# A retention and maxout kernel on one core: the first FFN products moved around block 3 of the start-up

## The chip, the cores and the metric

The kernel runs on one core of a Trainium2 chip. The metric is the device time of one execution in microseconds (us); the figure for a kernel is the median of its runs. Engines are named as in the profile: PE is TensorE (PEld its weight loads), DVE is VectorE, ACT is ScalarE, POOL is GpSimd, SP is SyncE, whose queue issues most of the transfers.

## The reference

Eight sequences of 576 tokens with eight heads of 64 go through causal retention (attention with a decay in place of the softmax); the result, 4608 tokens of 512 values, goes through a feed-forward network whose hidden layer is the maximum of three products.

```
scores = scale * q @ k^T                         # per batch and head
ret    = scores * (gamma ** (i - j) if i >= j else 0)
x      = (ret @ v), heads side by side           # 4608 x 512, float32
h      = max(x @ w1, x @ w2, x @ w3)             # w: 512 x 768, float64 from the host
out    = h @ w_out                               # 4608 x 512
```

## The kernel before

**Retention by blocks.** The 36 blocks of 128 tokens are worked through in order. For a block, `load(g)` fetches k, q and v; `decay(g)` multiplies v by the key decay on GpSimd (L249); `transposes(g)` makes kT and qT, for the first seven blocks by TensorE (L271) with a copy from PSUM by ScalarE (L272), later by VectorE; `scores(g)` is kT x qT on TensorE (L285) with a causal mask on VectorE; `state(g)` and `keep(g)` carry the sum of k x v from block to block (L352, L362, L363); `values(...)` is scores x v (L393) plus the part from the state (L406), scaled by the output factors `gq` and written to `xT` by VectorE. Blocks 8 and later use chunks of 64 tokens instead (L307, L310).

**The FFN by tiles of four blocks.** Tile t has 512 tokens (NT), `xT[t]`. The first tile is computed with plain products: `up_plain` (L784) is one of 18 products of 128 hidden columns, each with four sub-products over the depth; `i` = 0 is copied to `h` by ScalarE (L789), i = 1 and 2 are combined by a maximum on VectorE (L788). `downs_plain` (L771) is the output product. Later tiles use sums and differences of operands that save products (L748, L760, L557).

**Weights.** They come as 64-bit floats. `load_weights(1)` fetches one piece (128 hidden columns, 512 KB, two transfers; L499) into half of a `bits` buffer. `convert(n)` takes n steps of a generator that turns pieces into 32-bit floats, in steps named exponent, fraction, whole, sign and product, of which exponent and fraction have ScalarE parts (L632, L638, L641) and all have VectorE parts (L630, L639, L644, L648, L656). The first piece takes four steps, the second four. For the next pairs, up to the sixth piece, exponent and fraction of both pieces come before whole, sign and product. `product` ends by fetching one more piece.

**Order.** The schedule is manual: each engine gets its instructions in program order. At the end of the kernel's body the first four blocks stand written out by hand, with conversion steps between them; then, for every tile, a list of steps for the next tile's blocks alternates with parts of the FFN. From the second tile on, VectorE work for the coming blocks goes through a queue, `urgent`; the FFN takes entries from it at certain steps (L839, L840), and `scores` and `values` empty it before they begin. The hand-written order of loads at the start is:

```
k0 q0 v0  k1 q1 v1  (state factors gs)  k2 q2 v2  k3 q3  w0  v3  w1  k4 q4 v4  w2 w3 w4 w5
```

Of the kernel before, what the change touches and what calls it, by code (L numbers as in the profile page):

```python
# [45 lines left out]
ALU = mybir.AluOpType  # L46
PSUM = bass.MemoryType.PSUM

C = 128
NT = 4 * C  # L50
# [27 lines left out]
WAHEAD = 6  # L78
# [3 lines left out]
def kernel(  # L82
# [14 lines left out]
    nc = tc.nc  # L97
    P = 128
    B, H, S, D = q.shape
# [4 lines left out]
    NDC = DM // P  # L104
    NF = DF // P
    CPT = NT // C
# [8 lines left out]
    ppool = ctx.enter_context(tc.tile_pool(name="ppool", bufs=PARTS))  # L115
    opool = ctx.enter_context(tc.tile_pool(name="opool", bufs=2))
    while_converting = ExitStack()
    wraw = while_converting.enter_context(tc.tile_pool(name="wraw", bufs=WAHEAD // 2))
    wtmp = while_converting.enter_context(tc.tile_pool(name="wtmp", bufs=2))
    raw0 = while_converting.enter_context(tc.tile_pool(name="raw0", bufs=1))  # L120
    ps_r = ctx.enter_context(tc.tile_pool(name="ps_r", bufs=4, space=PSUM))
# [3 lines left out]

    gk = const.tile([C, H], FP32, name="gk")
    gs_of = const.tile([P, H], FP32, name="gs_of")
    gs = const.tile([P, NP], FP32, name="gs")  # L130
    one, top, inf, first = (const.tile([P, 1], FP32, name=n) for n in ("one", "top", "inf", "first"))
    const.tile([P, FILL // 4], FP32, name="fill")
    gq = const.tile([P, NP, C], FP32, name="gq")
    nc.scalar.dma_start(gk[:], key_decay)
    nc.vector.memset(one[:], 1.0)
    nc.scalar.copy(first[:], one[:])

# [11 lines left out]
    def warm(n):  # L149

        ps = ps_y.tile([P, P], FP32, tag="y", name="warm")
        for _ in range(n):
            nc.tensor.matmul(ps[:], lhsT=ident[:], rhs=ident[:], start=True, stop=True)
# [15 lines left out]
    def spans(g):  # L169

        row = 0
        while row < C:
# [1 line left out]
            n = min(C - row, S - pos)  # L174
            yield row, b, pos, n
            row += n

    def half(j):
        return slice(D * j, D * (j + 1))

    def place(g, c):

# [39 lines left out]
                        t[r:r + 32, :, e, :],  # L222
                        src[b, :, pos:pos + 32, 32 * a:32 * a + 32].rearrange("h p i -> p h i"))

    def load(g):
        if g >= BY_PE and ("q", g) not in raws:
            load_blocks(g, *range(C // 32))
        for n, src in (("k", k), ("q", q), ("v", v)) if g < BY_PE else (("k", k), ("v", v)):
            if n == "v" and g == CPT - 1:
                load_weights(1)  # L230
            bufs = {"k": 3, "q": 2, "v": 4}[n]
            pool, bufs = (raw0, 1) if n != "v" and g < BY_PE and g % (bufs + 1) == bufs else (raw, bufs)
            if n == "v":
                t = vpool.tile([C, H, D], FP32, tag="v", name="vraw")
            else:
                t = pool.tile([C, H, D], FP32, tag=n, name=n + "raw", bufs=bufs)
            raws[n, g] = t
            for row, b, pos, m in spans(g):
                nc.sync.dma_start(t[row:row + m], src[b, :, pos:pos + m, :].rearrange("h p d -> p h d"))
# [100 lines left out]
    def state_factors():  # L340
        for j in range(2):
            nc.scalar.copy(gs_of[half(0), j::2], gs[half(j)])
# [386 lines left out]
    def convert(n):  # L729
        for _ in range(n):  # L730
            next(converting, None)
# [44 lines left out]
                    nc.sync.dma_start(out[t * NT + m * P:t * NT + (m + 1) * P, :], osb[:])  # L776
            yield

    def up_plain(t, h, fb, i):
        ps = (ps_x, ps_y)[fb % 2].tile([P, NT], FP32, tag="xy"[fb % 2], name="up")  # L780
        first_of_all = t == 0 and (fb, i) == (0, 0)
        for cols in (slice(0, NT - C), slice(NT - C, NT)) if first_of_all else (slice(0, NT),):
            for dc in range(NDC):
                nc.tensor.matmul(ps[:, cols], lhsT=w_sb[i, fb][:, dc * P:(dc + 1) * P], rhs=xT[t][:, dc, cols],  # L784
                                 start=dc == 0 and cols.start == 0, stop=dc == NDC - 1,
                                 skip_group_check=first_of_all)
        if i > 0:
            return lambda: nc.vector.tensor_tensor(h[:, fb, :], h[:, fb, :], ps[:], op=ALU.max)  # L788
        return lambda: nc.scalar.copy(h[:, fb, :], ps[:])  # L789

    def ffn(t):

        h = hpool.tile([P, NF, NT], FP32, tag="h", name="h")
        if t == 0:
            for fp, i in units:
                for fb in (2 * fp, 2 * fp + 1):
                    maximum = up_plain(t, h, fb, i)
                    if CPT not in qks:
                        maximum()
                        transposes(CPT)  # L800
                        convert(4)
                        continue
                    if (fp, i) == units[-1]:
                        maximum()
                        convert(2)
                        continue
                    convert(4 if (fp, i) in units[:2] else 2)
                    maximum()
                yield
            convert(3)  # L810
            for fb, _ in enumerate(downs_plain(t, h)):
                convert(2 if fb < 2 else 4 * len(pieces))
                if fb == 2:
                    while_converting.close()
                    late["pool"] = ctx.enter_context(tc.tile_pool(name="late", bufs=1))
                    late_room()
                    sums_of_outs()
                elif fb > 2:
                    chore({3: 4, 4: 0, 5: 2}[fb])
                if fb in (1, 3):  # L820
                    yield
            yield
            return
        if t == 1:
            spread.append(True)
            weight_sums(0)
            weight_sums(2)
        plain = 1 if t == 1 else None
        order = (1, 0, 2) if t == 1 else (0, 2, 1)
        total = sum(48 if fp == plain else 2 * len(PRODUCTS) for fp in order)  # L830
        count = parts = 0
        for fp in order:
            if fp != plain:
                while fp not in summed_fp:
                    chore()
            for step, cost in enumerate(up_plain_all(t, h, fp) if fp == plain else up(t, h, fp)):
                if fp == plain:
                    chore(4 if step == 4 else 8)
                elif step % 4 == 1 or step % 4 == 3 and len(urgent) > 6:  # L839
                    chore(len(urgent) > 0)  # L840
                elif step % 4 == 2 and chores and (t > 1 or NF // 2 - 1 not in summed_fp):
                    chores.popleft()()
                if step % 3 == 2:
                    scale()
                count += cost or 1
                if count * (NF // 2 * 3) >= (parts + 1) * total:
                    parts += 1
                    yield
            sums_of_hidden(h, fp)
            if fp == plain:  # L850
                weight_sums(fp)
        chore(len(urgent))
        for n, _ in enumerate(downs(t, h, order)):
            chore(4)
            scale(2)
            if n in (1, 3):
                yield
        yield

    def up_plain_all(t, h, fp):  # L860
        for fb in (2 * fp, 2 * fp + 1):
            for i in range(3):
                up_plain(t, h, fb, i)()
                yield 8


    warm(6)
    for g in range(CPT):
        load(g)
        if g == 1:  # L870
            for j in range(2):
                nc.sync.dma_start(gs[half(j)].unsqueeze(2), state_decay[half(j), :, D * j:D * j + 1])
    load_weights(1)
    load(CPT)
    load_weights(4)
    decay(0)
    transposes(0)
    for c in range(2):
        for b in range(2):
            nc.scalar.dma_start(gq[half(c), b::2, :], out_decay[half(b), NP // 2 * c:NP // 2 * (c + 1), :])  # L880
    warm(2)
    scores(0)
    transposes(1)
# [4 lines left out]
    scores(1)  # L888
    first_output()
    transposes(2)  # L890
    state_factors()
    decay(2)
    state(1)
    keep(1)
    values([1], [1])
    transposes(3)
    decay(3)
    scores(2)
    scores(3)
    state(2)  # L900
    keep(2)
    convert(2)
    values([2], [2])
    convert(2)
    values([3], [3])
    convert(4)
    keep(3)
    decay(CPT)
    convert(2)

    def steps(t):

# [11 lines left out]
        if t == 1:  # L924
            a, b, c, d = range(CPT, 2 * CPT)
            at(0, (load, b))
            at(1, (scores, a), (state, a), (keep, a))
            at(2, (transposes, b), (decay, b), (load, c))
            at(3, (scores, b), (load_blocks, d, 0))
            at(4, (decay, c), (load_blocks, d, 1, 2))  # L930
            at(5, (values, [a, b], [b, c]), (load_blocks, d, 3), (load, d))
            at(6, (keep, c), (transposes, c), (load_blocks, d + 1, 0))
            at(7, (transposes, d), (decay, d), (load_blocks, d + 1, 1, 2))
            at(8, (scores, c), (scores, d), (load_blocks, d + 1, 3), (load, d + 1))
            at(9, (load_blocks, d + 2, 0, 1))
            at(10, (decay, d + 1), (load_blocks, d + 2, 2))
            at(11, (values, [c, d], [d]), (load_blocks, d + 2, 3), (load, d + 2),
               (transposes, d + 1))
            return todo
# [70 lines left out]
```

## Time and profile before

| | |
|---|---|
| Time, median of 3 | 756.83 us (756.58 to 757.96) |
| Profiled span | 754.8 us |
| TensorE busy | 745.0 us |
| VectorE busy | 509.2 us |
| ScalarE busy | 320.0 us |
| GpSimd busy | 83.3 us |
| First FFN product begins | 25.97 us |
| Granted TensorE clock | 1.00 |

Times in the profile count from the span's start. A line of the timeline has the start, the time to the end of the group, the engine, the line of the kernel, the operation with output and inputs, and how many instructions are joined; in square brackets stands how long the engine was idle before, and who released it. A line of the waits has the total in us, how often, and the longest.

### The profile page before, as it was taken

What the parts mean: (1) busy time and instruction counts of PE and PEld (TensorE: products, weight loads), DVE (VectorE), ACT (ScalarE), POOL (GpSimd) and SP (SyncE); (2) the same over time, 40 slices, a digit from 0 to 9 for tenths busy, and PEclk for the clock granted to TensorE, in tenths of its full rate; (3) what the DMA queues carried; (4) which work ended last, traced back from release to release, by engine and by line L of the source; (5) the groups of instructions that cost most, each with busy time, mean ns of one, the idle gap of its engine ahead of it and who ended that gap; (6) DMA issues with size and microseconds to landing.
All of it is one profiled execution on the core that took longest, in us unless ns stands there. A gap on an engine that the chain in (4) does not pass through costs nothing.

```text
span 754.8 us, 16567 instructions
## 1 busy us (share of the span) xinstructions
PE 745.0 (99%) x6728; PEld 608.2 (81%) x6728; DVE 509.2 (67%) x856; ACT 320.0 (42%) x645; POOL 83.3 (11%) x103
## 2 busy tenths in 40 slices
PE   8999999999999999999999999999999999999998
PEld 7645545588888888888888888888888888888887
DVE  2998896858876866677567647675667656763662
ACT  3574531064245443543355435542454245414441
POOL 3110112001000110011010101010101010100000
PEclk9999999999999999999999999999999999999999
DMA  9995842504241414342243324242415151000001
GB/s 218 254 216 125 234 98 69 100 2 77 66 102 40 85 44 100 56 73 55 69 88 63 65 61 95 33 81 63 87 38 96 43 97 32 1 30 29 0 1 56
DMA packets 230204, 59.30 MB, mean 79 GB/s; under 512 B 210800, under 2 KB 228848, under 8 KB 230128
## 3 DMA queue, kind: packets, MB, share of 16 engines
q1 hardware_dynamic: 229264, 57.91, 35.0%
q8 instruction: 53, 0.87, 0.5%
q10 hardware_dynamic: 864, 0.33, 0.2%
q14 instruction: 23, 0.19, 0.1%
HBM read 48.76 MB, written 9.44 MB: 77 GB/s over the span
## 4 chain that ended last, share of the span: by engine, by line
PE 96%; DVE 2%; DMA 1%; issue 0%; ACT 0%; POOL 0%; DVEq 0%; POOLq 0%
PE a L760 18%; PE b L760 15%; PE dx L557 11%; PE up L784 11%; PE c L760 8%; PE dz L557 5%; PE d L760 5%; PE e L760 5%; PE sk L307 3%; PE down L771 3%; PE dy L557 3%; PE o L424 2%; PE o L431 2%; PE s L285 1%; DMA qraw<-in_q_dram 1%; PE kv L310 1%
## 5 line engine op out<-in xcount | busy, mean ns | idle before, releaser
L748 DVE TENSOR_TENSOR part<-part 128x512 f32<-128x512 f32 x161 | 111.2, 691 | 108.4 <-ACT part L745 106.0
L745 ACT COPY part<-b 128x512 f32<-128x512 f32 x115 | 67.4, 586 | 154.8 <-PE b L760 154.8
L748 DVE TENSOR_TENSOR h<-h,part 128x512 f32<-128x512 f32 x115 | 80.3, 698 | 29.3 <-ACT h L745 25.4
L784 PE MATMUL up<-xT,w 128*128 128x512 f32 (+2 forms) x200 | 84.7, 578 | 1.5 <-DVE w L656 1.5
L745 ACT COPY part<-a 128x512 f32<-128x512 f32 x92 | 53.9, 586 | 49.0 <-PE a L760 48.5
L784 PEld LDWEIGHTS up<-xT,w 128*128 128x128 f32 x200 | 36.8, 190 | 43.5 <-issue 39.6
L760 PE MATMUL a<-s,w 128*128 128x256 f32 x276 | 70.9, 379 | 0.0
L760 PE MATMUL b<-s,n 128*128 128x256 f32 x276 | 70.8, 379 | 0.0
L189 ACT ACTIVATE vraw<-vraw,gk 128x64 f32<-128x64 f32 x208 | 65.7, 347 | 4.5 <-DMA vraw<-in_v_dram 4.4
L760 PEld LDWEIGHTS b<-s,n 128*128 128x128 f32 x276 | 52.4, 190 | 7.1
L760 PEld LDWEIGHTS a<-s,w 128*128 128x128 f32 x276 | 52.4, 190 | 7.1
L527 POOL TENSOR_TENSOR H<-h 128x256 f32<-128x256 f32 x24 | 20.2, 843 | 308.7 <-DVE h L748 308.7
L760 PE MATMUL c<-xT,w 128*128 128x256 f32 x184 | 49.1, 389 | 0.0
L760 PE MATMUL d<-s,w 128*128 128x256 f32 x184 | 47.3, 379 | 0.0
L760 PE MATMUL b<-xT,n 128*128 128x256 f32 x184 | 47.2, 379 | 0.0
L324 POOL TENSOR_TENSOR s<-s,gs_of 64x512 f32<-64x512 f32 x21 | 22.2, 1055 | 213.7 <-DVE s L322 209.1
L557 PE MATMUL dx<-To,H 128*128 128x256 f32 (+1 forms) x204 | 44.9, 370 | 0.0
L760 PE MATMUL e<-xT,w 128*128 128x256 f32 x184 | 43.5, 379 | 0.0
L760 PE MATMUL a<-xT,n 128*128 128x256 f32 x184 | 43.5, 379 | 0.0
L557 PEld LDWEIGHTS dx<-To,H 128*128 128x128 f32 x204 | 36.6, 190 | 4.9
L760 PEld LDWEIGHTS e<-xT,w 128*128 128x128 f32 x184 | 35.0, 190 | 5.2 <-DVE s L322 0.2
L760 PEld LDWEIGHTS d<-s,w 128*128 128x128 f32 x184 | 34.9, 190 | 4.9 <-ACT part L745 0.2
(122 smaller groups left out, 1287.2 us busy)
## 6 DMA issues: line engine op xcount, KB each, us to landing
bits<-in_moe_w_dram SPq DMA_DIRECT2D x36, 256.0 KB, 5.1
out_dram<-osb SPq DMA_DIRECT2D x35, 256.0 KB, 2.1
kraw<-in_k_dram SPq DMA_DIRECT2D x32, 256.0 KB, 3.0
vraw<-in_v_dram SPq DMA_DIRECT2D x32, 256.0 KB, 3.5
qraw<-in_q_dram SPq DMA_DIRECT2D x224, 32.0 KB, 2.1
kxraw<-in_k_dram SPq DMA_DIRECT2D x224, 32.0 KB, 2.1
bits<-in_moe_w_out_dram SPq DMA_DIRECT2D x6, 512.0 KB, 5.5
qraw<-in_q_dram SPq DMA_DIRECT2D x6, 256.0 KB, 5.2
```

The costliest lines, as they stand in the source:

```text
L189: scaling.popleft()()
L307: nc.tensor.matmul(s[half(c), h, :], lhsT=kT[half(c), h, :], rhs=qT[half(c), h, :], start=True, stop=True)
L324: nc.gpsimd.tensor_tensor(new, new, factor, op=ALU.mult)
L424: nc.tensor.matmul(o[m][half(c), n, u, :], lhsT=vds[g][half(m), h, :], rhs=sts[g][half(m), h, :], start=n == 0 and u == 0, stop=place(g, m ...
L431: nc.tensor.matmul(o[m][half(c), n, u, :], lhsT=stacks[g][half(m), h, :], rhs=qks[g]["q"][half(m), h, :], start=False, stop=True, skip_gro ...
L527: urgent.append(lambda: (pool(s3, a11, a21, op=ALU.subtract), pool(s4, a12, s2, op=ALU.subtract)))
L557: nc.tensor.matmul(o, lhsT=hS[n](fp)[:, m * P:(m + 1) * P], rhs=late["T"][n][:, fp, cols], start=first and fp == order[0] and (m == 0 or l ...
L745: nc.scalar.copy(of[step], ps[step[0]][:])
L748: nc.vector.tensor_tensor(of[dst], a, b, op=op)
L760: nc.tensor.matmul(ps[chain][:, e, :], lhsT=factor(w, 2 * fp + e), rhs=xS[t][x], start=n == 1 and e == 0, stop=ends, skip_group_check=True)
L771: nc.tensor.matmul(b[:], lhsT=h[:, fb, m * P:(m + 1) * P], rhs=w_sb["out", fb], start=(fb == 0), stop=(fb == NF - 1))
L784: nc.tensor.matmul(ps[:, cols], lhsT=w_sb[i, fb][:, dc * P:(dc + 1) * P], rhs=xT[t][:, dc, cols], start=dc == 0 and cols.start == 0, stop= ...
```

## The change

Part of the retention of block 3 is waited for at the start, and so is the first weight. The change loads the first two weight pieces before block 3's k and q and before its v, converts the first one during block 2, and puts the first 384 columns (tokens of blocks 0 to 2) of the first FFN product ahead of block 3's state and values and those of the second product behind them; the last 128 columns of both follow. The state factors are fetched on ScalarE's queue at the very beginning, and half of the output factors ahead of block 0's transposes. A fourth `bits` buffer takes two more pieces ahead. In the second tile, entries of `urgent` are taken at a further step while more than two are waiting (six before).

```diff
-    wraw = while_converting.enter_context(tc.tile_pool(name="wraw", bufs=WAHEAD // 2))
+    wraw = while_converting.enter_context(tc.tile_pool(name="wraw", bufs=WAHEAD // 2 + 1))
     nc.scalar.dma_start(gk[:], key_decay)
+    for j in range(2):
+        nc.scalar.dma_start(gs[half(j)].unsqueeze(2), state_decay[half(j), :, D * j:D * j + 1])
...
+    def first_ups(h):
+        g = CPT - 1
+        rest0, copy0 = up_plain(0, h, 0, 0, g * C)
+        convert(2)
+        state(g)
+        values([g])
+        keep(g)
+        rest1, copy1 = up_plain(0, h, 1, 0, g * C)
+        for step in (rest0, copy0, rest1, copy1):
+            step()
+        decay(CPT)
+        transposes(CPT)
+        convert(10)
...
-                elif step % 4 == 1 or step % 4 == 3 and len(urgent) > 6:
+                elif step % 4 == 1 or step % 4 == 3 and len(urgent) > (2 if t == 1 else 6):
...
-    for g in range(CPT):
+    for g in range(CPT - 1):
         load(g)
-        if g == 1:
-            for j in range(2):
-                nc.sync.dma_start(gs[half(j)].unsqueeze(2), state_decay[half(j), :, D * j:D * j + 1])
     load_weights(1)
+    load(CPT - 1, "kq")
+    load_weights(1)
+    load(CPT - 1, "v")
+    load_weights(2)
     load(CPT)
-    load_weights(4)
+    load_weights(2)
     decay(0)
+    output_factors(0)
     transposes(0)
+    output_factors(1)
...
     transposes(2)
-    state_factors()
     decay(2)
     state(1)
     keep(1)
     values([1], [1])
-    transposes(3)
-    decay(3)
     scores(2)
-    scores(3)
+    decay(CPT - 1)
     state(2)
     keep(2)
+    convert(3)
+    values([2], [2])
+    transposes(CPT - 1)
+    convert(1)
+    state_factors()
     convert(2)
-    values([2], [2])
-    convert(2)
-    values([3], [3])
-    convert(4)
-    keep(3)
-    decay(CPT)
-    convert(2)
+    scores(CPT - 1)
...
-            at(2, (transposes, b), (decay, b), (load, c))
+            at(2, (transposes, b), (decay, b), (load, c), (load_weights, 2))
```

In the old order the first tile's FFN began with the whole first product, then block 4's transposes, then the second product.

More of the change, by code (lines that the diff above doesn't have):

```diff
@@ L124, with half @@
     ctx.enter_context(tc.manual_schedule())
+    def half(j):
+        return slice(D * j, D * (j + 1))
     gk = const.tile([C, H], FP32, name="gk")
@@ L176, in spans @@
             row += n
-    def half(j):
-        return slice(D * j, D * (j + 1))
     def place(g, c):
@@ L223, in load_blocks, with load @@
                         src[b, :, pos:pos + 32, 32 * a:32 * a + 32].rearrange("h p i -> p h i"))
-    def load(g):
+    def load(g, names="kqv"):
         if g >= BY_PE and ("q", g) not in raws:
@@ L228, in load @@
         for n, src in (("k", k), ("q", q), ("v", v)) if g < BY_PE else (("k", k), ("v", v)):
-            if n == "v" and g == CPT - 1:
-                load_weights(1)
+            if n not in names:
+                continue
             bufs = {"k": 3, "q": 2, "v": 4}[n]
@@ L777, in downs_plain, with up_plain, products, maximum @@
             yield
-    def up_plain(t, h, fb, i):
+    def up_plain(t, h, fb, i, *parts):
         ps = (ps_x, ps_y)[fb % 2].tile([P, NT], FP32, tag="xy"[fb % 2], name="up")
-        first_of_all = t == 0 and (fb, i) == (0, 0)
-        for cols in (slice(0, NT - C), slice(NT - C, NT)) if first_of_all else (slice(0, NT),):
+        def products(a, b):
             for dc in range(NDC):
[L784 to L789, printed above, removed]
+                nc.tensor.matmul(ps[:, a:b], lhsT=w_sb[i, fb][:, dc * P:(dc + 1) * P], rhs=xT[t][:, dc, a:b],
+                                 start=dc == 0 and a == 0, stop=dc == NDC - 1, skip_group_check=len(parts) > 0)
+        def maximum():
+            if i > 0:
+                nc.vector.tensor_tensor(h[:, fb, :], h[:, fb, :], ps[:], op=ALU.max)
+            else:
+                nc.scalar.copy(h[:, fb, :], ps[:])
+        ends = [0, *parts, NT]
+        steps = [partial(products, a, b) for a, b in zip(ends, ends[1:])]
+        steps.pop(0)()
+        return (*steps, maximum)
+    def first_ups(h):
[11 more added lines that the diff above has]
+        convert(10)
     def ffn(t):
@@ L795, in ffn @@
             for fp, i in units:
+                if (fp, i) == units[0]:
+                    first_ups(h)
+                    yield
+                    continue
                 for fb in (2 * fp, 2 * fp + 1):
[L797 to L800, printed above, removed]
-                        convert(4)
-                        continue
+                    maximum, = up_plain(t, h, fb, i)
                     if (fp, i) == units[-1]:
@@ L805, in ffn @@
                         convert(2)
-                        continue
-                    convert(4 if (fp, i) in units[:2] else 2)
-                    maximum()
+                    else:
+                        convert(4 if (fp, i) == units[1] else 2)
+                        maximum()
                 yield
@@ L862, in up_plain_all, with output_factors @@
             for i in range(3):
-                up_plain(t, h, fb, i)()
+                maximum, = up_plain(t, h, fb, i)
+                maximum()
                 yield 8
     warm(6)
-    for g in range(CPT):
+    for g in range(CPT - 1):
         load(g)
-        if g == 1:
-            for j in range(2):
-                nc.sync.dma_start(gs[half(j)].unsqueeze(2), state_decay[half(j), :, D * j:D * j + 1])
     load_weights(1)
+    load(CPT - 1, "kq")
+    load_weights(1)
+    load(CPT - 1, "v")
+    load_weights(2)
     load(CPT)
-    load_weights(4)
+    load_weights(2)
     decay(0)
-    transposes(0)
-    for c in range(2):
+    def output_factors(c):
         for b in range(2):
             nc.scalar.dma_start(gq[half(c), b::2, :], out_decay[half(b), NP // 2 * c:NP // 2 * (c + 1), :])
+    output_factors(0)
+    transposes(0)
+    output_factors(1)
     warm(2)
@@ L895 @@
     values([1], [1])
-    transposes(3)
-    decay(3)
     scores(2)
-    scores(3)
+    decay(CPT - 1)
     state(2)
     keep(2)
-    convert(2)
-    values([2], [2])
-    convert(2)
-    values([3], [3])
-    convert(4)
-    keep(3)
-    decay(CPT)
-    convert(2)
+    convert(3)
[3 more added lines that the diff above has]
+    state_factors()
+    convert(2)
+    scores(CPT - 1)
     def steps(t):
```

## The prediction

> **What bounds the kernel now.** I read the page's busy shares and the chain first, then the waits of TensorE, and then the timeline of each engine around the waits that were found.
>
> ```profile
> PE 745.0 (99%) x6728; PEld 608.2 (81%) x6728; DVE 509.2 (67%) x856; ACT 320.0 (42%) x645; POOL 83.3 (11%) x103
> ...
> PE 96%; DVE 2%; DMA 1%; issue 0%; ACT 0%; POOL 0%; DVEq 0%; POOLq 0%
> ```
>
> TensorE is the bound: 745.0 of 754.8 us busy, 96% of the chain. An edit that leaves its products alone, as this one does, can only change the time by the places where TensorE stands still. The waits of PE name all of them:
>
> ```profile
> PE qt L271 <- DMA qraw<-in_q_dram: 2.0, 2, 1.2
> PE up L784 <- DVE w L656: 1.5, 1, 1.5
> PE warm L153 <- POOL ident masks.py:199: 1.4, 1, 1.4
> PE down L771 <- DVE w_out L656: 1.1, 1, 1.1
> PE sk L307 <- DVE qT L194: 1.0, 1, 1.0
> ```
>
> The first two lie before 26 us, the fourth at 100 us, the fifth at 174 us. The reader is to see how little there is: 2.0 + 1.5 in the start, 1.1 and 1.0 later; the warm-up's 1.4 isn't touched. The start in order (PE's timeline; start us, us, what):
>
> ```profile
> 14.20 1.05 PE L393 MATMUL o<-st,vd 128*64 128x128 f32 x16
> 15.17 0.67 PE L406 MATMUL o<-qT,state 64*64 64x128 f32 x16
> 15.77 0.66 PE L271 MATMUL kt<-ident,kraw 128*128 128x128 f32 x4
> 17.66 0.63 PE L271 MATMUL qt<-ident,qraw 128*128 128x128 f32 x4 [1.23 <-DMA qraw<-in_q_dram]
> 18.21 2.06 PE L285 MATMUL s<-qT,kT 64*128 64x128 f32 x32
> 25.97 3.74 PE L784 MATMUL up<-xT,w 128*128 128x384 f32 x16 [1.48 <-DVE w L656]
> ```
>
> Block 3's q holds up the scores of blocks 2 and 3 together until 18.2, and the first FFN product waits until 25.97 for the first converted weight. And ScalarE and VectorE behind the transposes of block 4, which decide my forecast:
>
> ```profile
> 31.95 0.57 ACT L789 COPY h<-up 128x512 f32<-128x512 f32 x1
> 32.42 0.59 ACT L272 COPY kT<-kt 128x512 f32<-128x512 f32 x1
> 32.90 0.60 ACT L272 COPY qT<-qt 128x512 f32<-128x512 f32 x1
> 33.38 0.78 ACT L632 ACTIVATE mant<-bits,one 128x512 f32<-128x512 uint32 x1
> 34.06 0.71 ACT L638 ACTIVATE expo<-expo,top 128x512 f32<-128x512 int32 x1
> 34.80 0.72 ACT L641 ACTIVATE expo<-expo,inf 128x512 int32<-128x512 f32 x1
> ```
>
> ```profile
> 35.55 0.69 DVE L648 SCALAR_TENSOR_TENSOR expo<-bits,expo 128x512 int32<-128x512 int32 x1 [0.21 <-ACT expo L641]
> 36.28 0.69 DVE L656 TENSOR_TENSOR w<-mant,expo 128x512 f32<-128x512 f32 x1
> ```
>
> From the start of the qT copy (32.90) to the end of the weight whose conversion comes next on ScalarE (36.28 + 0.69 = 36.97) are 4.07 us. Here nobody waited: the piece that TensorE wanted at 35.65 had had its ScalarE steps before the copies.
>
> [...] the h copy above starts at 31.95, though its product ended near 29.7, because it stands behind two conversion steps. [...] In the trace the two state-factor issues take 1.59 us of SyncE's queue (5.90 to 7.5), for 1 KB each. [...] the w_out product before the down projection takes 1.95 us beside a GpSimd decay of 1.61, elsewhere 1.23 and 1.04.
>
> **The change, part by part.**
>
> *State factors to ScalarE's queue, half the output factors earlier.* Takes 1.59 us from SyncE ahead of block 2, so block 2's k is issued at 5.9 in place of 7.54. Against it, 128 KB of output factors now run among block 0's and 1's loads: at the 230 GB/s of 5 to 10 us that is 0.56 us. ScalarE's first copy waits until 5.25 anyway, so the issues hide before it unless they wait themselves. Gain at block 2 about 0.5 us, loss at block 1 between 0 and 0.6; I take 0.2 lost. Then block 2's transposes no longer wait, and block 1's values start when their masked scores are there: st at 11.79 + 1.29 = 13.1, not 14.20. Values and state part take 1.57 (14.20 to 15.77), so block 2's scores can start at 13.1 + 1.6 + 0.2 = 14.9.
>
> *The new order up to block 3.* Scores to values take 2.6 us through VectorE's mask (6.96 to 9.61 for block 0): values of block 2 at 17.5, of which some 0.9 is idle, since only the 0.6 of the kv product lies there. Values and state part 1.6 (20.73 to 22.33): block 3's transposes at 19.1. Its q, behind 512 KB of weights, should land near 18.5 (17.66 before, + 2 transfers of about 1 us, - 0.7 for the state factors). It is no longer the last wait. Transposes 1.04 (29.54 to 30.58), copy 0.59, some 0.15 to start: block 3's scores at 20.9, to 22.0, and TensorE idles 0.75 there.
>
> *First weight early, products in parts.* The first piece's conversion starts on VectorE after block 2's state, at 17.8 in place of 22.14; it took 3.8 us (22.14 to 25.91), so it is ready by 21.7, ahead of 22.0. The wait of 1.48 is gone. Then 384 columns (25.97 to 28.7) 2.7, kv 0.56, values 0.93, state part 0.6, second product's 384 columns 2.65, the two remainders 0.95 each: 9.3 us, so block 4's transposes start at 31.3.
>
> *What is given back.* In the old order a whole product lay between block 4's transposes and its scores. Now the scores follow at once: 1.04 + 0.59 + 0.15, 0.75 of it idle. And `convert(10)` stands after the transposes, while only eight conversion steps (the first two pieces) stand before: all ScalarE steps of the third piece queue behind the qT copy. That copy starts at 31.3 + 1.15 = 32.45, the piece is ready 4.07 later at 36.5, and the product begins at 36.55. Scores and kv (1.7 us) end by 34.8, so TensorE waits 1.75. Before, this product began at 35.65: **the start ends 0.9 later**. The gaps removed (0.78, 1.23, 1.48) come back as 0.9 + 0.75 + 0.75 + 1.75, against some 0.5 more of copy and mask latency that the old gaps didn't show.
>
> *Afterwards.* VectorE is 97% busy from 30 to 58, and conversion is late by about 1.5; the tightest piece was ready at 58.06 for a product at 58.5, so 0.1 more is lost. **Start: +1.0.**
>
> *Fourth bits buffer, two pieces more ahead.* SyncE waits less for buffers (4.4 us of waits on the sign step now, in which block loads queue behind it), and the last w_out bits come earlier. No gap of TensorE hangs on it except through block 8's v: its GpSimd decay at 98.28 lengthens the w_out product by 0.72. If it comes earlier it hits less. Between 0 and -0.7; I take -0.25. The rest of the 1.1 at 100 us moves with TensorE.
>
> *More urgent steps in the second token tile.* The 1.04 at 174 us is for block 11's qT, pushed out just before the scores: seven steps, one in four FFN products' steps of 1.73 us. With two per four until two are left it is issued near 168. **-1.04.** The cost, VectorE's joins later by a step of 0.7, has idle of 1.5 to 3.5 us beside it there.
>
> Sum: 756.83 + 1.0 - 0.25 - 1.04 = 756.5.
>
> **Rivals.** *Faster*: the third piece is not waited for, since ScalarE gets through earlier than I reckon, or the start runs ahead by as much elsewhere. For it: three waits of 3.5 us are removed. [...] It gives 1.75 less at the start, w_out's full 0.7: 756.5 - 1.75 - 0.45 = 754.3. *Slower*: transfers take the place of the waits removed. Weights stand ahead of block 3, ScalarE's first conversion step waits for them with block 3's copies behind it, and ScalarE's queue has four issues of 0.6 to 0.9 ahead of block 0's copies. For it: DMA is over 100% busy from 5 to 20 us. Against it: I find a microsecond of slack at each. One more us at the start, 0.25 not gained, 0.9 of the second tile's gap replaced: 758.65.
>
> **How the numbers follow.** The forecast (gain at 174 us cancels a loss at the start) gets 0.55, the faster case 0.28, the slower 0.17. The bound of 0.2% is 1.5 us, so these are same, faster and slower. For the range both neighbours' values are taken in: 754.4 to 758.7; costs bounded above (0 to 0.6, 0 to 0.7) lie within it.
>
> **What would show it.** Right: first FFN product near 22, TensorE waiting 1.5 to 2 us for w (L656's successor) near 35, the third piece's product begun near 36.5, no wait for qT at 174. Wrong: the third piece's product before 35, or after 37.5; a DMA wait of TensorE in the first 22 us; a new wait in the second tile.

## The result, and the profile after

The changed kernel takes 759.26 us (757.96 to 759.47, six runs) beside 756.44 for the kernel before in the same comparison: a ratio of 1.0031, 95% interval 1.0018 to 1.0044. It is slower, by 2.3 us by the ratio and 2.8 by the medians, and outside the forecast range. The profiled execution has a span of 757.1 us (754.8 before).

From the page of the changed kernel, the busy times, and the granted clock (one digit for each fortieth of the span, in tenths of full speed, where 9 is nine tenths or more; the kernel before has nines throughout):

```profile
PE 748.3 (99%) x6736; PEld 609.8 (81%) x6736; DVE 508.2 (67%) x856; ACT 319.5 (42%) x645; POOL 82.4 (11%) x103
...
PEclk9989999999999999999999999999999999999999
```

TensorE is busy for 3.3 us more, with eight more instructions among 6,700, and one slice, the third (38 to 57 us), isn't granted the full clock. So the loss isn't waiting alone: TensorE took longer over its products. The waits of PE:

```profile
PE s L287 <- ACT qT L274: 1.7, 3, 0.8
PE up L786 <- DVE w L658: 1.7, 1, 1.7
PE warm L158 <- POOL ident masks.py:199: 1.4, 1, 1.4
PE down L773 <- DVE w_out L658: 0.3, 1, 0.3
PE o L395 <- DVE st L203: 0.3, 2, 0.2
PE qt L273 <- DMA qraw<-in_q_dram: 0.3, 1, 0.3
```

Of the waits of before, 1.5 for the first weight, 2.0 for block 2's and 3's q and 1.0 for qT at 174 us are gone; the 0.3 for a q is block 1's. In their place stand 1.7 for the third piece's weight and 1.7 for q copies. PE's timeline shows where, and something that no line of waits shows:

```profile
21.42 1.16 PE L287 MATMUL s<-qT,kT 64*128 64x128 f32 x16 [0.73 <-ACT qT L274]
22.51 2.85 PE L786 MATMUL up<-xT,w 128*128 128x384 f32 x8
...
32.28 0.60 PE L273 MATMUL qt<-ident,qraw 128*128 128x128 f32 x4
33.66 1.16 PE L287 MATMUL s<-qT,kT 64*128 64x128 f32 x16 [0.78 <-ACT qT L274]
34.75 0.68 PE L354 MATMUL kv<-vd,kraw 64*64 64x64 f32 x16
37.13 10.16 PE L786 MATMUL up<-xT,w 128*128 128x512 f32 x16 [1.70 <-DVE w L658]
```

The first FFN product begins at 22.51, as forecast (near 22; 25.97 before). But the sixteen products from 37.13 on, pieces three and four, take 10.16 us; the same sixteen took 7.13 in the kernel before:

```profile
35.65 7.13 PE L784 MATMUL up<-xT,w 128*128 128x512 f32 x16
```

A table of the changed kernel by stretches (start:end, length, then busy us of PE, PEld, DVE, ACT, POOL, the granted clock, DMA share, GB/s) gives the reason:

```profile
33.00:35.00 2.00, 1.34 (x24) 1.22 (x26) 0.69 (x1) 1.97 (x5) 0.00 (x0) 1.00 1.11 261
35.00:37.00 2.00, 0.43 (x16) 0.29 (x11) 1.31 (x3) 1.97 (x4) 0.00 (x0) 0.85 1.26 249
37.00:39.00 2.00, 1.87 (x3) 0.84 (x4) 1.97 (x4) 1.29 (x2) 0.00 (x0) 0.50 1.00 245
39.00:41.00 2.00, 2.00 (x4) 0.97 (x3) 2.00 (x6) 1.51 (x3) 0.68 (x1) 0.50 1.07 243
41.00:43.00 2.00, 2.00 (x3) 0.72 (x3) 2.00 (x5) 1.87 (x3) 0.37 (x1) 0.50 1.07 271
43.00:45.00 2.00, 2.00 (x6) 0.78 (x5) 1.97 (x4) 1.30 (x2) 0.00 (x0) 0.94 1.11 274
```

From within 35 to 37 us until just after 43, TensorE was granted half its clock: three or four records in two microseconds in place of six. In the stretch just before it was busy for 1.34 and 0.43 of 2 us.

**Where the time went**, by how much later than before the same work begins. The third piece's product: 37.13 against 35.65, +1.48. Block 5's transposes behind pieces three and four: 47.12 against 42.62, +4.50, so half the clock cost 3.02 (by the table it lasted some 6.8 us). The first output product: 104.78 against 101.03, +3.75, since 0.76 of the wait there (1.10, now 0.34) went. The output products of the second tile: 190.87 against 188.54, +2.33, since the wait of 1.04 at 174 us went, with 1.42 in all. From there on the two run alike, and 2.3 is the difference of the spans. This execution is one of three of the six runs with a mean granted clock of 0.995; the other three have 0.998, so there the clock will have cost about half as much (an estimate from the mean clocks).

### The profile page after: what moved, and what is told of

The parts are those of the page before. It is cut to its first block, busy times and chain, and to the rows that moved or that the text cites. A ratio compares the mean times of both kernels' runs of the same rounds, so it can differ in the third digit from the quotient of the medians.

```text
span 757.1 us, 16577 instructions
## 1 busy us (share of the span) xinstructions
PE 748.3 (99%) x6736; PEld 609.8 (81%) x6736; DVE 508.2 (67%) x856; ACT 319.5 (42%) x645; POOL 82.4 (11%) x103
## 4 chain that ended last, share of the span: by engine, by line
PE 97%; DMA 1%; ACT 1%; DVE 1%; issue 0%; DVEq 0%
PE a L762 18%; PE b L762 16%; PE dx L559 11%; PE up L786 11%; PE c L762 8%; PE dz L559 5%; PE e L762 5%; PE d L762 5%; PE sk L309 3%; PE down L773 3%; PE dy L559 3%; PE o L426 2%; PE o L433 2%; PE o L395 1%; PE s L287 1%; PE kv L312 1%
## 5 line engine op out<-in xcount | busy, mean ns | idle before, releaser
L786 PE MATMUL up<-xT,w 128*128 128x512 f32 (+2 forms) x208 | 87.9, 579 | 1.7 <-DVE w L658 1.7
L786 PEld LDWEIGHTS up<-xT,w 128*128 128x128 f32 x208 | 38.8, 195 | 45.1 <-issue 40.3
L762 PEld LDWEIGHTS a<-xT,n 128*128 128x128 f32 x184 | 35.0, 190 | 4.8
```

Of the source, the lines that this page charges most:

```text
L762: nc.tensor.matmul(ps[chain][:, e, :], lhsT=factor(w, 2 * fp + e), rhs=xS[t][x], start=n == 1 and e == 0, stop=ends, skip_group_check=True)
L786: nc.tensor.matmul(ps[:, a:b], lhsT=w_sb[i, fb][:, dc * P:(dc + 1) * P], rhs=xT[t][:, dc, a:b], start=dc == 0 and a == 0, stop=dc == NDC - ...
```

## The experiments

Two theories stood against each other. A: the half clock follows from TensorE standing still between 32.9 and 37.1 us, and the cause of both is that the third piece's ScalarE steps queue behind the q copy. B: the half clock has another cause in the new order, such as its smaller products.

### Filling the idle time: e1_fill

```diff
         transposes(CPT)
+        warm(2)
         convert(10)
...
+                if (fp, i) == units[1]:
+                    warm(7)
                 for fb in (2 * fp, 2 * fp + 1):
```

> The changed kernel with two idle-filling products of the identity behind block 4's transposes and seven ahead of the third weight piece's product (results unused), so that TensorE has work in its 0.78 and 1.70 us of waiting; nothing else moves. Theory A (the half clock from 36.4 to 43.3 us follows from TensorE standing still between 32.9 and 37.1): no half clock, the third piece's product still begins near 37.1, block 5's transposes near 44.1 in place of 47.1, about 756.3 us. Theory B (the half clock has another cause, such as the smaller products of the new order): half clock as before, 759.3 us.

Measured: 757.32 us, ratio to the kernel before 1.0012 (1.0006 to 1.0019), and the full clock in all 21 runs. PE's timeline of this kernel:

```profile
35.40 1.83 PE L158 MATMUL warm<-ident 128*128 128x128 f32 x14
37.17 7.13 PE L786 MATMUL up<-xT,w 128*128 128x512 f32 x16
44.14 0.60 PE L273 MATMUL kt<-ident,kraw 128*128 128x128 f32 x4
...
54.25 4.13 PE L786 MATMUL up<-xT,w 128*128 128x512 f32 x9 [1.11 <-DVE w L658]
```

The third piece's product begins where it did (37.17 against 37.13), the sixteen products take 7.13 again, and block 5's transposes come at 44.14: theory A, to a tenth of a microsecond. Useless work made the kernel 1.4 us faster by the ratios, 1.9 by the medians. It isn't the whole 3.0, but that is the cost in an execution at 0.995; with three of six runs at 0.998, some 2.4 us are to be expected (an estimate: the mean of 3.0 and of 1.7, which the clock in e4_after_urgent6's trace gives for half as long a stretch). The 756.3 that theory A was given was too low by 1.0.

The wait of 1.11 for a weight at 54 us belongs to this execution, one of the two slowest of the 21. The weight's last step on VectorE met a decay on GpSimd and took 1.95 us. In the profiled execution of e6_fill_second, the next experiment, it took 1.23, and there is no such wait. GpSimd and VectorE here, then VectorE there:

```profile
51.54 1.57 POOL L251 TENSOR_TENSOR vd<-vraw,gk 128x512 f32<-128x512 f32 x1 [11.49 <-DMA vraw<-in_v_dram]
...
52.25 1.95 DVE L658 TENSOR_TENSOR w<-mant,expo 128x1024 f32<-128x1024 f32 x1
```

```profile
51.72 1.23 DVE L658 TENSOR_TENSOR w<-mant,expo 128x1024 f32<-128x1024 f32 x1
```

### How much idle is enough: e6_fill_second, e9_fill_two, e10_fill_four

The same without the `warm(2)` behind block 4's transposes, and with `warm(7)`, `warm(2)` or `warm(4)` ahead of the third piece.

> The changed kernel with the seven filling products ahead of the third piece's product alone, the 0.78 us behind block 4's transposes left empty. If the 1.70 us is the idle stretch that brings the half clock: full clock throughout, 757.3 us as with both filled. If [...] the small products count as idle too: half clock as in the changed kernel, 758 to 759.3 us.

> As with seven filling products, but two: some 0.45 of the 1.70 us filled, 1.25 left, besides the 0.78. If the half clock needs the whole stretch of idle: full clock, 757.2 us. If 1.25 + 0.78 us of idle are enough: half clock in some or all runs, 758 to 759.3 us.

> As with seven filling products, but four: some 0.9 us filled, 0.8 left, besides the 0.78. Full clock, 757.2 us, if no more idle is needed than that for it to stay; half clock and 758 to 759.3 us if the sum of 1.6 us is too much.

Measured: 757.13, 757.13 and 757.53 us (ratios 1.0009, 1.0007 and 1.0013). The three profiled executions have the full clock, and the mean granted clock was never under 0.999 in the runs of the three. With two filling products the timeline has

```profile
33.11 1.16 PE L287 MATMUL s<-qT,kT 64*128 64x128 f32 x16 [0.78 <-ACT qT L274]
34.20 0.68 PE L354 MATMUL kv<-vd,kraw 64*64 64x64 f32 x16
34.82 0.71 PE L158 MATMUL warm<-ident 128*128 128x128 f32 x4
36.59 3.70 PE L786 MATMUL up<-xT,w 128*128 128x512 f32 x8 [1.06 <-DVE w L658]
```

So behind 0.78 and 1.06 us of standing still, with 2.4 of work between, the clock was 1.00; behind 0.78 and 1.70, with 1.8 between, it was 0.50. Filling the wait for the weight was enough, and so was cutting it by over a third. A kernel that fills the 0.78 and keeps the 1.70 wasn't run, so whether the 0.78 counts as well stays open, and nothing between 1.06 and 1.70 was run.

### Taking the cause away: e2_early

```diff
         rest0, copy0 = up_plain(0, h, 0, 0, g * C)
-        convert(2)
+        convert(6)
         state(g)
...
         transposes(CPT)
-        convert(10)
+        convert(6)
```

> The changed kernel with the exponent and fraction steps of the third and fourth weight pieces (four conversion steps) moved from behind block 4's transposes to ahead of block 3's state, so that their ScalarE part isn't queued behind the q copy. Theory A: the wait of 1.70 us ahead of the third piece's product goes, and with it the half clock: product near 35.5, about 754.5 us, under the kernel before. Theory B (half clock from another cause): the wait goes, the half clock stays, about 757.5 us. A third way: the new weights haven't landed by 26 us, VectorE waits for them with block 3's output behind it, and the first products' last columns come later by as much.

Measured: 755.01 us (754.38 to 755.74, 17 runs), ratio 0.9982 (0.9975 to 0.9989): faster than the kernel before, and by about 4 us than the changed kernel. ScalarE's timeline of this kernel, beside that of the changed one:

```profile
24.71 0.79 ACT L634 ACTIVATE mant<-bits,one 128x512 f32<-128x512 uint32 x1 [1.46 <-DMA bits<-in_moe_w_dram]
26.47 0.72 ACT L640 ACTIVATE expo<-expo,top 128x512 f32<-128x512 int32 x1 [0.96 <-DVE expo L632]
27.22 0.72 ACT L643 ACTIVATE expo<-expo,inf 128x512 int32<-128x512 f32 x1
```

```profile
33.01 0.60 ACT L274 COPY qT<-qt 128x512 f32<-128x512 f32 x1
33.48 0.78 ACT L634 ACTIVATE mant<-bits,one 128x512 f32<-128x512 uint32 x1
34.14 0.73 ACT L640 ACTIVATE expo<-expo,top 128x512 f32<-128x512 int32 x1
34.91 0.72 ACT L643 ACTIVATE expo<-expo,inf 128x512 int32<-128x512 f32 x1
```

The changed kernel's ScalarE does nothing for 7.32 us up to 31.15, and takes up the third piece behind the copies at 33.48. In the new version the third piece's steps are done by 28, in that idle time; the weights land at 24.7, early enough. The third piece's product then begins at 34.79 behind the kv product without a wait, and the sixteen products run at the full clock:

```profile
34.79 7.13 PE L786 MATMUL up<-xT,w 128*128 128x512 f32 x16
```

Of the 2.34 us by which it begins earlier than in the changed kernel, 1.70 are the wait; 0.58 were there already at block 2's scores (15.08 against 15.66), where the two kernels are still alike.

### Block 4's transposes under a product: e5_early_t4

On top of early conversion:

```diff
-        for step in (rest0, copy0, rest1, copy1):
-            step()
+        rest0()
+        copy0()
         decay(CPT)
         transposes(CPT)
+        rest1()
+        copy1()
         convert(6)
```

> The kernel of early conversion, with block 4's decay and transposes between the last columns of the first and of the second product. My theory (each microsecond of TensorE's waiting at the start that goes is a microsecond of the time, as long as conversion keeps up): 0.95 us of product now covers the qT copy, the wait of 0.78 goes, about 754.3 us. Rival: VectorE's conversion has become the limit; the time stays at 755.0 us and a wait for w comes up between 50 and 60 us.

Measured: 754.16 us (753.64 to 754.6), ratio 0.9967 (0.9955 to 0.998). PE's timeline:

```profile
31.18 0.60 PE L273 MATMUL qt<-ident,qraw 128*128 128x128 f32 x4
31.61 1.06 PE L786 MATMUL up<-xT,w 128*128 128x128 f32 x8
32.60 1.16 PE L287 MATMUL s<-qT,kT 64*128 64x128 f32 x16
```

The second product's last columns cover the q copy, the 0.78 is gone, and no wait for w comes up later. This is the fastest of the kernels by its ratio, 1.1 us under early conversion, though from five runs and with intervals that overlap. Part of it may be chance: of the 1.2 us between the two profiled spans, 0.8 lie in the wait ahead of the output products (0.3 against 1.1), which changes between executions, as the last experiments show. The idea of the change works once conversion is placed to go with it.

### The second tile's threshold alone: e3_before_urgent2, e4_after_urgent6

```diff
-                elif step % 4 == 1 or step % 4 == 3 and len(urgent) > 6:
+                elif step % 4 == 1 or step % 4 == 3 and len(urgent) > (2 if t == 1 else 6):
```

> The kernel before, with only the threshold of the urgent queue in the second tile changed from 6 to 2. My theory: the wait of 1.04 us for block 11's qT goes, worth 1.0 to 1.4 us: about 755.2 us. Rival: the gain seen in the second tile comes from other parts of the change (transfers or buffers a little earlier), and the time stays within 0.3 us.

> The changed kernel with the threshold back at 6. My theory: the wait for block 11's qT comes back, 1.0 to 1.4 us more than the changed kernel, about 760.5 us. Rival: no difference.

Measured: the kernel before with this line alone takes 755.22 us, ratio 0.9983 (0.9975 to 0.9992), 1.05 less than the 756.27 of its comparison, and its trace has no wait for qT in the second tile. The changed kernel without it takes 759.33, ratio 1.0041 (1.0028 to 1.0053), beside 1.0031 (1.0018 to 1.0044) with it: the expected side, with intervals that overlap. Its waits show the 1.0 back, with the third piece's wait beside it:

```profile
PE up L786 <- DVE w L658: 1.7, 1, 1.7
...
PE sk L309 <- DVE qT L196: 1.0, 1, 1.0
```

### Factors and buffers: e7_old_factors, e8_three_bits

Both on top of early conversion: the state factors on SyncE's queue behind block 1 again, with all output factors behind block 0's transposes; and three bits buffers, without `(load_weights, 2)`.

> The kernel of early conversion with the state factors back on SyncE's queue behind block 1 and all output factors behind block 0's transposes. My theory: what moving them gains at block 2 it loses at blocks 0 and 1, within 0.4 us of 755.0. Rival: SyncE's 1.6 us of issuing is worth that much at block 2's scores and all that follows: 756 to 756.6 us.

> The kernel of early conversion with three bits buffers in place of four, and without the two extra pieces in the second step. My theory: no product waits for the bits, only block 8's v shifts against the w_out product, within 0.7 us of 755.0. Rival: the weights come too late without the fourth buffer, a wait for w of a microsecond or more between 35 and 60 us, 756 us or more.

Measured: 755.14 us (ratio 0.9979, 0.9971 to 0.9987) and 755.26 us (0.9984, 0.9977 to 0.9992), beside 755.01 (0.9982). Neither part is worth anything that can be told from these times. The profiled execution with the old factors does show a cost: block 1's scores wait 0.80 us for their q copy, and block 2's scores begin at 16.10. (In the trace of the kernel before, with the same order on ScalarE, it issues the output factors for 3.21 us from 6.22 on, and block 1's first copy comes behind them, at 9.47.) In five other versions with the new order, which are alike up to there, block 2's scores begin between 15.08 (early conversion) and 15.66 (the changed kernel), so the start varies by about as much from one execution to the next. The kernel before, with the old order of issues, shows both: no such wait in its own profiled execution, one of 0.8 for a q copy in that of e3_before_urgent2. A gain of half a microsecond from the move is neither shown nor excluded.

The wait ahead of the output products, which I had linked to the buffer through block 8's v, goes its own way: 1.1 us with four buffers (early conversion) and with three; 1.1 in the kernel before and 0.3 in it with the threshold alone, which acts only later; 0.3 in the changed kernel and 1.2 in e4_after_urgent6, which are alike up to there too. VectorE and GpSimd in early conversion, and then in the kernel with the threshold alone:

```profile
97.97 1.04 POOL L251 TENSOR_TENSOR vraw<-vraw,gk 128x512 f32<-128x512 f32 x1 [11.88 <-DMA vraw<-in_v_dram]
...
98.13 1.96 DVE L658 TENSOR_TENSOR w_out<-mant,expo 128x1024 f32<-128x1024 f32 x1
```

```profile
99.51 1.23 DVE L656 TENSOR_TENSOR w_out<-mant,expo 128x1024 f32<-128x1024 f32 x1
...
100.06 1.58 POOL L249 TENSOR_TENSOR vraw<-vraw,gk 128x512 f32<-128x512 f32 x1 [15.27 <-DMA vraw<-in_v_dram]
```

In both, whichever starts first runs at its own length (1.04 or 1.23) and the other takes longer (1.96, 1.58). So it is in e8_three_bits, where GpSimd begins at 98.46 with 1.04 and VectorE at 98.58 with 2.01, and in e5_early_t4, where VectorE begins at 97.65 with 1.22 and GpSimd at 97.75 with 2.03. Which one it is hangs here on when v lands, 0.16 us ahead of VectorE's step in early conversion and 0.55 behind its start in the other trace, and isn't a property of the change.

## Why the prediction was wrong

**The step that failed is "What is given back".** It counted TensorE's standing still at its own length. It named the wait and nearly its size (1.75 expected, 1.70 measured, the copies first and the third piece's three ScalarE steps behind them, exactly as in the trace), and took for granted that TensorE goes on at full speed afterwards. The same premise stands at its head: an edit that leaves the products alone could change the time only where TensorE stands still. It didn't go on at full speed: some 6.8 us at half clock cost 3.02, which the sum had at nothing. e1_fill shows it by filling the wait, e2_early by removing it. The profile of before showed nine tenths or more everywhere, which told me only that its own waits, of at most 1.48, had come without a half clock in that execution.

**The start: +0.9 forecast, +1.48 measured.** The mechanism was right. The missing 0.6 stands in one term: block 2's scores begin at 15.66, not 14.9, in this execution. Block 1's q was waited for by 0.27, its scores came 0.36 later, and with them block 1's mask and values (13.92 in place of 13.3). The terms behind that, from block 2's scores to the third piece, were forecast at 21.65 us and took 21.47. The balance of gaps given with the forecast doesn't close: 4.15 come back for 3.49 removed, which is 0.66; the 0.9 rests on the start times. Nor is the wait for the first weight gone in every execution: that of e6_fill_second, the same kernel up to there, has 0.37 of it.

**Afterwards, +0.1 for late conversion.** In the changed kernel it can't be seen: TensorE at half clock asked for its weights later. With the full clock e1_fill waits 1.11 and some 0.2 for later weights and e9_fill_two some 0.5, but e6_fill_second and e10_fill_four not at all. So lateness alone isn't shown to cost more than the 0.1; what the term left out is the longer step beside a GpSimd decay, 0.72 in one step of e1_fill (1.95 against 1.23).

**The second tile, -1.04.** Right in kind: -1.42 between the traces, -1.05 by the medians for the line alone. The queue is emptied later than I reckoned, though: block 11's qT comes at 176.4, just ahead of its scores, not near 168 + 3.75.

**The output products, -0.25 with a bound of -0.7.** It was -0.76 in the profiled execution, but by the luck of when a transfer lands.

**Factors and buffers.** Little was forecast, and e7_old_factors and e8_three_bits find nothing that can be told from the times.

With the clock's 3.0 in the sum, the forecast of 756.5 would have been 759.5. That this lies so near the 759.26 is in part luck: the errors of the other terms, +0.6 at the start, -0.5 ahead of the output products and -0.4 in the second tile, nearly cancel. The slower rival, 758.65, gave another cause, transfers in the place of the waits removed: this isn't what happened. TensorE's one DMA wait in the profiled start was 0.3 us.

## What to carry to other kernels

When work is moved to fill a wait, look at what it had been hiding: here a product that covered a copy, and conversion steps that had stood ahead of that copy on ScalarE (in the kernel before the steps end at 32.05 and the q copy begins at 32.90; in the changed one the q copy begins at 33.01 and the steps at 33.48). Count a new wait of TensorE at its length, and then look at the granted clock behind it: in the profiled executions a wait of 1.70 us brought another 3.0, and one of 1.06 brought nothing. A wait that can't be removed can be filled with useless products, as in e1_fill, where 1.83 us of them stand ahead of the third piece and the clock stays at 1.00. And where a bundle comes out worse, its parts may still be good: this one, with conversion steps and block 4's transposes moved, makes a kernel 0.33% faster than the one before.

## What the runs showed of the hardware

Behind two waits, of 0.78 and 1.70 us with 1.8 us of work between, TensorE's clock in the changed kernel was 0.50; with the second filled (e6_fill_second) or gone (e2_early) it was 1.00. In the profiled execution the half clock lasted some 6.8 us (by the table in the section on the result). In that of e4_after_urgent6 it lasted half as long, by the granted clocks of this table, which come to 1.70 us lost (an estimate: 0.33, 0.50 and 0.02 of two microseconds each):

```profile
37.00:39.00 2.00, 1.93 (x3) 0.91 (x4) 1.97 (x5) 1.25 (x2) 0.00 (x0) 0.67 0.82 182
39.00:41.00 2.00, 2.00 (x4) 0.71 (x3) 2.00 (x6) 1.56 (x3) 0.94 (x1) 0.50 1.02 252
41.00:43.00 2.00, 2.00 (x6) 0.97 (x5) 2.00 (x5) 1.90 (x4) 0.10 (x1) 0.98 0.95 220
```

The half clock doesn't come in every run: the mean granted clock was 0.995 in three of the changed kernel's runs and 0.998 in three, and in e4's five it was 0.998 in three and 1.0 in two. Those two took 759.09 and 759.71 us, within the 759.04 to 760.31 of the other three, which isn't explained.

The kernel before isn't free of a lower clock either. In the three comparisons of the experiments, 9 of its 121 runs have a mean clock of 0.997 or 0.998, and their median is 758.13 us, against 756.36 for the 109 at 1.0. What brings it there no trace shows.
